# Fetching an expert's rows: one whole-row gather and a TensorE transpose, in place of four quarter-row gathers and a VectorE transpose

## The chip, the cores and the metric

The kernel runs on one core of one Trainium2 chip. The metric is the device time of one execution in microseconds (us). A profile is taken of a separate execution of the same program; its times are counted from the first instruction of that execution.

## What is computed

Three stages follow each other: attention, a gated mlp, and a mixture of eight experts of which every token uses two. The change touches only the way in which the third stage gets its rows. Cut to what matters:

```python
x = attention(q, k, v)                              # 2304 tokens x 512
x = (silu(x @ w_gate) * (x @ w_val)) @ w_out        # gated mlp, 512 -> 1536 -> 512
noisy = x @ g_gate + log1p(exp(x @ g_noise)) * noise
top2, top2_w = the two largest of 8 per token, softmax of the two
for e in range(8):
    for k in range(2):
        mask = top2[:, k] == e
        h = maximum(x[mask] @ w1[e], 0)             # 512 -> 1024
        out[mask] += top2_w[mask, k] * (h @ w2[e])  # 1024 -> 512
```

## The kernel before

TensorE (PE) multiplies in float32r. For the accuracy of float32 every operand is split into a high and a low part (`split`, L397: ScalarE copies the high part, VectorE subtracts it from the source for the low part), and three of the four products are summed (`PASSES`, L459).

The gated mlp goes through 6 blocks of 384 tokens and 12 chunks of 128 hidden columns (the loop at L763). Attention and the routing of finished blocks are woven between its matmuls. `m_evac` (L499) scales a finished block and writes its rows to the DRAM tensor `x1d`; ScalarE writes them with the columns permuted (L505). `routing` (L519) computes the gates of a block, gives each token a slot for each of its two experts, and scatters token number and weight to the DRAM list `slotd` (L607). Blocks 0 to 4 are read back from `x1d` in quarters and transposed by VectorE (`quarters`, L513); the last block is still in SBUF and is transposed by TensorE (L528), four 128x128 transposes a tile.

The experts follow (L818 on). Each has 5 tiles of 128 slots (`CAPT`): a group of 3 and a group of 2 (`GN`). A unit is one expert, one group and one of 8 hidden chunks: 16 units an expert, 128 in all. In a unit TensorE does 12 matmuls of `x_h` (L820) for its own chunk and then those of `x_o` (L835) for the chunk before: 9 with three tiles, 6 with two. A finished group is scaled and added to `out` by an indirect DMA a tile (L847).

The rows of expert e+1 are fetched while expert e is multiplied. Counted in units of expert e: at 0 `load_info` reads the slot list from DRAM; at 2 `info` turns it into row numbers; at 3 to 7 `gather` (L699) fetches one tile each; at 10 to 14 `xtrans` (L707) transposes one tile each and splits it into `XG`, which `x_h` reads. Experts 0 and 1 are fetched in part before the last block has been routed (`early_steps`, L746), and their fifth tile at the end of it (L879). Expert 7 has no expert after it, so nothing is gathered while it runs.

Transposing a tile by 32x32 blocks, as VectorE does, is a whole transpose only if each quarter of the columns stands in its own 32 partitions. So `gather` sees `x1d` as four times as many rows of 128 columns (`x1q`, L66) and fetches each tile in four indirect DMAs, with row numbers 4 x token + quarter (`idq`, L693), which need a list of their own in another layout (`inq`, four DMAs at L685). Where a line says `pin`, the instruction is kept behind everything that its engine was given before; the others may be moved by the compiler's scheduler.

The indirect DMAs are issued by GpSimd (POOL), plain loads by SyncE (SP). TensorE, VectorE (DVE) and ScalarE (ACT) each take their instructions in order.

Of the kernel before, what the change touches and what calls it, by code (L numbers as in the profile page):

```python
# [8 lines left out]
F32 = mybir.dt.float32  # L9
F32R = mybir.dt.float32r  # L10
BF16 = mybir.dt.bfloat16
I32 = mybir.dt.int32
U32 = mybir.dt.uint32
AF = mybir.ActivationFunctionType
OP = mybir.AluOpType
# [6 lines left out]
def attention_moe_kernel(ctx: ExitStack, tc: tile.TileContext, q, k, v, w_gate, w_val, w_out,  # L22
# [42 lines left out]
    x1d = dram.tile([NT + PAD, DM], F32, name="x1d")  # L65
    x1q = x1d.rearrange("t (a c) -> (t a) c", a=4)  # L66
    slotd = dram.tile([E * REG, 2], F32, name="slotd")
# [28 lines left out]
    iota8 = const.tile([P, E], F32, name="iota8")  # L96
    quad4 = const.tile([P, 1], F32, name="quad4")
    payload = const.tile([P, NTILE, 2, 2], F32, name="payload")
# [9 lines left out]
    def more_consts():  # L108
        for a in range(4):
            nc.gpsimd.memset(quad4[a * ST:(a + 1) * ST], float(a))  # L110
        nc.gpsimd.memset(wgn, 0.0)
        nc.gpsimd.memset(up, 1.0)
        sel(up, [[1, P]], 0, -1, 0.0, OP.is_gt)
        nc.gpsimd.memset(ones, 1.0)
        nc.gpsimd.iota(iota8, pattern=[[1, E]], base=0, channel_multiplier=0,
                       allow_small_or_imprecise_dtypes=True)
        nc.gpsimd.iota(payload[:, :, :, 0], pattern=[[P, NTILE], [0, 2]], base=PAD, channel_multiplier=1,
                       allow_small_or_imprecise_dtypes=True)
        nc.gpsimd.iota(base, pattern=[[REG, E]], base=0, channel_multiplier=0,
                       allow_small_or_imprecise_dtypes=True)  # L120
        nc.gpsimd.iota(basea, pattern=[[REG, E]], base=NTA, channel_multiplier=0,
                       allow_small_or_imprecise_dtypes=True)
        ini = hp_.tile([P, NROW, 2], F32, name="ini", tag="x1", bufs=X1B)
        inits.append(ini)
        inii = hp_.tile([P, NROW], I32, name="inii", tag="xf", bufs=3)
        nc.gpsimd.iota(inii, pattern=[[1, NROW]], base=0, channel_multiplier=NROW % PAD)
        nc.vector.tensor_scalar(inii, inii, PAD - 1, None, op0=OP.bitwise_and)
        nc.vector.memset(ini, 0.0)
        nc.vector.tensor_copy(ini[:, :, 0], inii)
# [18 lines left out]

    # ------------------------------------------------------------- attention + gated mlp
    p1 = ctx.enter_context(ExitStack())  # L150
# [122 lines left out]

    # local heads: a tile holds 64 queries of two heads, one under the other
    def a_scores(qd):
# [117 lines left out]

    # ---- weights of the gated mlp, as exact sums of two float32r parts
    W = {}
# [103 lines left out]
    def m_evac(j):  # L499
        for t in range(3):  # L500
            if j == NBLK - 1:
                x = p2a[0].tile([P, DM], F32, name="xrow", tag="xrow", bufs=6)
            else:
                x = hp_.tile([P, DM], F32, name="x1", tag="x1", bufs=X1B)
            nc.scalar.mul(x.rearrange("p (a m j) -> p m a j", a=4, j=ST),  # L505
                          ACC[j][t].rearrange("p (m a j) -> p m a j", a=4, j=ST), 0.5)
            r0 = PAD + (3 * j + t) * P
            nc.scalar.dma_start(out=x1d[r0:r0 + P, :], in_=x)
            if j == NBLK - 1:
                X1[j, t] = x  # L510

    # rows of x1 with a quarter of the columns to each 32 partitions, transposed by blocks
    def quarters(dst, src):  # L513
# [5 lines left out]
    def routing(j):  # L519
        L = rt.tile([P, 3, 2 * E], F32, name="L", tag="L", bufs=2)  # L520
        pl = at_tile("ps_l", 3, P)
        for t in range(3):
# [15 lines left out]
            for kk in range(KD):  # L538
                nc.tensor.matmul(pl[kk * ST:(kk + 1) * ST, t, :], wgn[:, j == NBLK - 1, kk, :], xt[:, kk, :],
                                 start=True, stop=True)  # L540
# [129 lines left out]
    GN, GT = (3, 2), (0, 3)  # L670
    INFO, IDX, IDQ, XG, XR, WX = {}, {}, {}, {}, {}, {}
    p2a, p2b = [None], [None]
# [4 lines left out]
    def load_info(e, t0, t1):  # L677
# [4 lines left out]
        nc.sync.dma_start(out=inf[:, :n, :], in_=slotd[r0:r0 + n * P, :].rearrange("(t p) c -> p t c", p=P))  # L682
        inq = rt.tile([P, 4 * CAPT], F32, name="inq", tag="inq", bufs=2)
        for a in range(4):
            nc.sync.dma_start(out=inq[a * ST:(a + 1) * ST, :4 * n],  # L685
                              in_=slotd[r0:r0 + n * P, 0:1].rearrange("(g i) o -> i (g o)", i=ST))
        LI[e, t0] = inf, ids, inq, n

    def info(e, t0):
        inf, ids, inq, n = LI.pop((e, t0))  # L690
        idq = rt.tile([P, 4 * CAPT], I32, name="idq", tag="idq", bufs=3)
        pin(nc.vector.tensor_copy(ids[:, :n], inf[:, :n, 0]))
        pin(nc.vector.tensor_scalar(idq[:, :4 * n], inq[:, :4 * n], 4.0, quad4, op0=OP.mult, op1=OP.add))  # L693
        for t in range(t0, t0 + n):
            IDQ[e, t] = idq[:, 4 * (t - t0):4 * (t - t0 + 1)]
            INFO[e, t] = inf[:, t - t0, :]
            IDX[e, t] = ids[:, t - t0:t - t0 + 1]

    def gather(e, t, rows=NT):  # L699
        x = p2a[0].tile([P, 4, P], F32, name="xrow", tag="xrow", bufs=6)  # L700
        for g in range(4):
            nc.gpsimd.indirect_dma_start(  # L702
                out=x[:, g, :], out_offset=None, in_=x1q[:4 * (PAD + rows), :],
                in_offset=bass.IndirectOffsetOnAxis(ap=IDQ[e, t][:, g:g + 1], axis=0))
        XR[e, t] = x

    def xtrans(e, t):  # L707
# [5 lines left out]
        hi, lo = XG[e, g][:, :, 0, c0:c0 + P], XG[e, g][:, :, 1, c0:c0 + P]  # L713
        xt = hp_.tile([P, KD, P], F32, name="xgT", tag="xf", bufs=3)
        pin(quarters(xt, x))
        split(hi, lo, xt)

# [45 lines left out]
    for i, (j, c) in enumerate(seq):  # L763
# [37 lines left out]
        pend.append((j, c))  # L801
    # ------------------------------------------------------------- experts
    for _ in early[0]:
# [71 lines left out]
    def route_step():  # L875
# [6 lines left out]
        if rts and next(rts[0], "end") == "end":  # L882
# [3 lines left out]
            late.append(0)  # L886
            # tiles of slots that each expert needs
            cnt = rt.tile([P, E], F32, name="cnt")
# [25 lines left out]

    # ------------------------------------------------------------- what the static slots don't hold
    ov = ctx.enter_context(tc.tile_pool(name="ov", bufs=1, reuse_waits="tile"))
    worst = nc.values_load(ntile[0:1, E:E + 1], min_val=0, max_val=NTILE)
    with tc.If(worst > CAPT):
        for e in range(E):
            last = nc.values_load(ntile[0:1, e:e + 1], min_val=0, max_val=NTILE)  # L920
            with tc.For_i(CAPT, last, 1) as t:
# [7 lines left out]
                                             in_offset=bass.IndirectOffsetOnAxis(ap=ids, axis=0))  # L929
                xn = ov.tile([P, DM], F32, name="o_xn")  # L930
                nc.vector.tensor_copy(xn.rearrange("p (m a j) -> p m a j", a=4, j=ST),
                                      x.rearrange("p (a m j) -> p m a j", a=4, j=ST))
                ps = ps_at.tile([P, DM], F32, name="o_ps", tag="at")
                for kk in range(KD):
                    nc.tensor.transpose(ps[:, kk * P:(kk + 1) * P], xn[:, kk * P:(kk + 1) * P], ident)
                xt = ov.tile([P, DM], F32, name="o_xt")
# [47 lines left out]
```

## Time and profile before

| what | us |
|---|---|
| device time, median of 3 runs | 1088.91 (1087.77 to 1089.51) |
| span of the profiled execution (no other time of it is given) | 1189.3 |
| TensorE matmuls busy in it | 1079.4 (91%) |
| VectorE busy | 580.1 (49%) |
| ScalarE busy | 439.4 (37%) |
| GpSimd busy | 366.0 (31%) |
| last matmul ends at; from there to the end of the span | 1175.5; 13.8 |

The span of the profiled execution is 100.4 us longer than the median of the timed ones, so an idle stretch in the profile need not be there in the time. The page has the busy time of each engine, the span in 40 slices, the DMA queues, the chain of work that ended last, and the costliest groups of instructions; the trace behind it answers for a line, a tile, or a stretch of time. Busy times of TensorE have modelled ends, and consecutive matmuls overlap in them: the step from one start to the next is what one costs in a stream.

### The profile page before, as it was taken

The numbers are of one execution on the slowest core, as the hardware profiler recorded it, in microseconds if no ns is written. First come the engines' busy times: TensorE is split into PE (matmuls) and PEld (weight loads), VectorE is DVE, ScalarE is ACT, GpSimd is POOL, SyncE is SP. The second block draws the span as 40 slices with busy tenths as digits, with TensorE's granted clock in tenths as the row PEclk, the third lists the DMA queues.
The fourth block names the chain that finished last, engine by engine and source line by source line (L and its number), as shares of the span: only waits on it lengthen the run. The fifth ranks groups of instructions, "written<-read, shape, count | busy, mean of one in ns | idle before, by whom it ended". The sixth has DMA issues, their size and how long they took to land.

```text
span 1189.3 us, 17431 instructions
## 1 busy us (share of the span) xinstructions
PE 1079.4 (91%) x6262; PEld 935.6 (79%) x6268; DVE 580.1 (49%) x1524; ACT 439.4 (37%) x1099; POOL 366.0 (31%) x418
## 2 busy tenths in 40 slices
PE   7988799999999999999889688897979799897995
PEld 4667688988888888898878577796969688696994
DVE  5879885555556645535455162341606153250511
ACT  4645454245444534434333141331505042241410
POOL 5136420311212300200343616234252615334211
PEclk8989899999999999999989889898979999898998
DMA  8666763565426313114452254351715444351412
GB/s 170 157 181 184 207 166 95 87 210 140 74 60 131 49 49 96 40 45 147 90 164 72 41 128 97 77 140 36 180 42 142 85 103 115 58 160 31 63 14 35
DMA packets 187154, 123.65 MB, mean 104 GB/s; under 512 B 96225, under 2 KB 154081, under 8 KB 187057
## 3 DMA queue, kind: packets, MB, share of 16 engines
q1 hardware_dynamic: 168256, 92.22, 30.2%
q0 software_dynamic: 16208, 25.49, 11.7%
q10 hardware_dynamic: 2592, 4.72, 1.1%
q8 instruction: 51, 0.84, 0.3%
q14 instruction: 47, 0.38, 0.1%
HBM read 98.04 MB, written 24.30 MB: 103 GB/s over the span
## 4 chain that ended last, share of the span: by engine, by line
PE 29%; issue 13%; DMA 3%; POOL 3%; another core or an unknown queue 1%; DVE 1%; SPq 1%; ACT 0%; POOLq 0%; DVEq 0%; ACTq 0%
PE acc L835 14%; PE ps_h L820 14%; POOL xrow L702 2%; DMA out_dram<-y,ids 2%; DMA slotd<-payload,si 1%; POOL slotd L607 1%; DMA raw<-in_moe_w_dram 0%; POOL out_dram L847 0%; SPq L685 0%; PE ps_g L467 0%; PE ps_v L467 0%; DVE W L399 0%; DVE wohl L399 0%; DMA inf<-slotd 0%
## 5 line engine op out<-in xcount | busy, mean ns | idle before, releaser
L835 PE MATMUL acc<-W,hhl 128*128 128x512 f32 x960 | 262.3, 417 | 39.2 <-issue 34.4
L820 PE MATMUL ps_h<-xg,W 128*128 128x256 f32 (+1 forms) x1536 | 260.0, 316 | 21.7 <-issue 21.7
L820 PEld LDWEIGHTS ps_h<-xg,W 128*128 128x128 f32 x1536 | 244.4, 194 | 38.3 <-issue 26.8
L835 PEld LDWEIGHTS acc<-W,hhl 128*128 128x128 f32 x960 | 187.0, 202 | 76.6 <-issue 37.9
L824 DVE SCALAR_TENSOR_TENSOR hhl<-ps_h,hhl 128x256 fp32r<-128x256 f32 (+1 forms) x128 | 61.5, 480 | 297.0 <-ACT hhl L823 207.3
L702 POOL DMA_INDIRECT xrow<-x1d,idq x160 | 154.0, 963 | 102.2 <-issue 55.8
L467 PE MATMUL ps_g<-xh,W 128*128 128x384 f32 x864 | 170.8, 345 | 5.9 <-DVE th L475 5.9
L823 ACT ACTIVATE hhl<-ps_h 128x256 fp32r<-128x256 f32 (+1 forms) x128 | 55.8, 436 | 323.9 <-PE ps_h L820 145.7
L467 PE MATMUL ps_v<-xh,W 128*128 128x384 f32 x864 | 168.9, 343 | 5.1 <-DVE th L482 5.1
L494 PE MATMUL acc<-wohl,hhl 128*128 128x512 f32 x648 | 171.3, 405 | 0.0
L467 PEld LDWEIGHTS ps_g<-xh,W 128*128 128x128 f32 x864 | 152.9, 191 | 13.9 <-DVE th L475 6.5
L467 PEld LDWEIGHTS ps_v<-xh,W 128*128 128x128 f32 x864 | 152.3, 190 | 8.0 <-DVE th L482 3.7
L847 POOL DMA_INDIRECT out_dram<-y,ids x40 | 62.9, 1573 | 257.6 <-ACT y L846 234.8
L494 PEld LDWEIGHTS acc<-wohl,hhl 128*128 128x128 f32 x648 | 120.4, 191 | 25.4 <-issue 3.0
L398 ACT CAST W<-raw 128x512 fp32r<-128x512 f32 x128 | 76.2, 618 | 59.2 <-PE acc L835 36.1
L399 DVE TENSOR_TENSOR W<-raw,W 128x512 fp32r<-128x512 f32 x128 | 85.4, 687 | 25.2 <-ACT W L398 14.6
L607 POOL DMA_INDIRECT slotd<-payload,si x36 | 36.3, 1010 | 130.5 <-DVE si L594 100.4
L398 ACT CAST hhl<-th 128x384 fp32r<-128x384 f32 x72 | 36.9, 513 | 96.7 <-DVE th L482 95.1
L227 POOL DMA_DIRECT2D v<-in_v_dram x28 | 19.4, 695 | 165.9 <-PE ps_o L332 153.4
L475 DVE SCALAR_TENSOR_TENSOR th<-th,ps_g 128x384 f32<-128x384 f32 x72 | 39.7, 551 | 51.7 <-ACT th L474 43.9
L474 ACT ACTIVATE th<-ps_g 128x384 f32<-128x384 f32 x72 | 35.3, 490 | 79.7 <-PE ps_g L467 69.9
L304 ACT ACTIVATE sc<-sc,mn 126x126 f32<-126x126 f32 (+3 forms) x152 | 56.5, 374 | 20.8 <-DVE mn L301 20.6
(136 smaller groups left out, 1018.9 us busy)
## 6 DMA issues: line engine op xcount, KB each, us to landing
raw<-in_moe_w_dram SPq DMA_DIRECT2D x128, 256.0 KB
raw<-wod SPq DMA_DIRECT2D x60, 256.0 KB
raw<-in_moe_w_gate_dram SPq DMA_DIRECT2D x12, 512.0 KB
raw<-in_moe_w_val_dram SPq DMA_DIRECT2D x12, 512.0 KB
raw<-in_moe_w_out_dram SPq DMA_DIRECT2D x12, 512.0 KB
out_dram<-zero SPq DMA_DIRECT2D x20, 256.0 KB
x1d<-x ACTq DMA_DIRECT2D x15, 256.0 KB
xq<-x1d SPq DMA_DIRECT2D x60, 64.0 KB
```

Source lines behind the costliest of these rows:

```text
L304: nc.scalar.activation(s[:n, i, :m], s[:n, i, :m], AF.Exp, bias=mn[:n, i:i + 1], scale=-1.0, accum_out=rs[:n, i])
L398: nc.scalar.copy(dst_hi, src)
L399: (eng or nc.vector).tensor_tensor(dst_lo, src, dst_hi.bitcast(F32), op=OP.subtract)
L467: nc.tensor.matmul(ps, W[c][:, o + a, kk * P:(kk + 1) * P], XH[j, kk][:, b2, :], start=(kk == KORD[0] and a == 0 and b2 == 0), stop=(kk == ...
L494: nc.tensor.matmul(ACC[j][t], h[:, a, t * P:(t + 1) * P], wo[:, b2, :], start=(c == 0 and a == 0 and b2 == 0), stop=(c == NC1 - 1 and a == 1))
L607: s = nc.gpsimd.indirect_dma_start(out=slotd, out_offset=bass.IndirectOffsetOnAxis(ap=si[:, t, i:i + 1], axis=0), in_=pay[:, t, i, :], in_ ...
L702: nc.gpsimd.indirect_dma_start(out=x[:, g, :], out_offset=None, in_=x1q[:4 * (PAD + rows), :], in_offset=bass.IndirectOffsetOnAxis(ap=IDQ[ ...
L820: nc.tensor.matmul(ps, w[:, a, kk * P:(kk + 1) * P], XG[e, g][:, kk, b2, :], start=(kk == 0 and a == 0 and b2 == 0), stop=(kk == KD - 1 an ...
L823: nc.scalar.activation(h[:, 0, :n], ps, AF.Relu)
L824: nc.vector.scalar_tensor_tensor(h[:, 1, :n], ps, 0.0, h[:, 0, :n].bitcast(F32), op0=OP.max, op1=OP.subtract)
L835: nc.tensor.matmul(ACC2[e, g][t], h[:, a, t * P:(t + 1) * P], w[:, 2 + b2, :], start=(c == 0 and a == 0 and b2 == 0), stop=(c == NC2 - 1 a ...
L847: s = nc.gpsimd.indirect_dma_start(out=out, out_offset=bass.IndirectOffsetOnAxis(ap=IDX[e, ti], axis=0), in_=y, in_offset=None, compute_op ...
```

## The change

`x1d` now holds plain rows. `gather` fetches the 128 rows of a tile whole, 2 KB each, in one indirect DMA, with the token numbers that `info` already makes for the scatter. `xtrans` transposes the tile on TensorE, four 128x128 transposes into one PSUM bank, pinned behind what TensorE was given before; `split` then reads PSUM in place of SBUF. The second list (`inq`, `idq`, `quad4`) and its DMAs are gone. The two layouts of the gate weights (`wgn`) change places, because the read-back of blocks 0 to 4 in quarters now meets plain rows and the last block's too are plain. The branch for slots beyond five tiles (L918 on) loses a copy. The diff, without comment lines:

```diff
-    x1q = x1d.rearrange("t (a c) -> (t a) c", a=4)
...
@@ m_evac
-            nc.scalar.mul(x.rearrange("p (a m j) -> p m a j", a=4, j=ST),
-                          ACC[j][t].rearrange("p (m a j) -> p m a j", a=4, j=ST), 0.5)
+            nc.scalar.mul(x, ACC[j][t], 0.5)
@@ routing
-                nc.tensor.matmul(pl[kk * ST:(kk + 1) * ST, t, :], wgn[:, j == NBLK - 1, kk, :], xt[:, kk, :],
+                nc.tensor.matmul(pl[kk * ST:(kk + 1) * ST, t, :], wgn[:, j < NBLK - 1, kk, :], xt[:, kk, :],
@@ load_info
-        inq = rt.tile([P, 4 * CAPT], F32, name="inq", tag="inq", bufs=2)
-        for a in range(4):
-            nc.sync.dma_start(out=inq[a * ST:(a + 1) * ST, :4 * n],
-                              in_=slotd[r0:r0 + n * P, 0:1].rearrange("(g i) o -> i (g o)", i=ST))
-        LI[e, t0] = inf, ids, inq, n
+        LI[e, t0] = inf, ids, n
@@ info
-        idq = rt.tile([P, 4 * CAPT], I32, name="idq", tag="idq", bufs=3)
         pin(nc.vector.tensor_copy(ids[:, :n], inf[:, :n, 0]))
-        pin(nc.vector.tensor_scalar(idq[:, :4 * n], inq[:, :4 * n], 4.0, quad4, op0=OP.mult, op1=OP.add))
@@ gather
-        x = p2a[0].tile([P, 4, P], F32, name="xrow", tag="xrow", bufs=6)
-        for g in range(4):
-            nc.gpsimd.indirect_dma_start(
-                out=x[:, g, :], out_offset=None, in_=x1q[:4 * (PAD + rows), :],
-                in_offset=bass.IndirectOffsetOnAxis(ap=IDQ[e, t][:, g:g + 1], axis=0))
+        x = p2a[0].tile([P, DM], F32, name="xrow", tag="xrow", bufs=6)
+        nc.gpsimd.indirect_dma_start(out=x, out_offset=None, in_=x1d[:PAD + rows, :],
+                                     in_offset=bass.IndirectOffsetOnAxis(ap=IDX[e, t], axis=0))
@@ xtrans
-        xt = hp_.tile([P, KD, P], F32, name="xgT", tag="xf", bufs=3)
-        pin(quarters(xt, x))
-        split(hi, lo, xt)
+        ps = at_tile("ps_xg", KD, P)
+        for m in range(KD):
+            pin(nc.tensor.transpose(ps[:, m, :], x[:, m * P:(m + 1) * P], ident))
+        split(hi, lo, ps)
@@ the branch for slots beyond five tiles
-                xn = ov.tile([P, DM], F32, name="o_xn")
-                nc.vector.tensor_copy(xn.rearrange("p (m a j) -> p m a j", a=4, j=ST),
-                                      x.rearrange("p (a m j) -> p m a j", a=4, j=ST))
...
-                    nc.tensor.transpose(ps[:, kk * P:(kk + 1) * P], xn[:, kk * P:(kk + 1) * P], ident)
+                    nc.tensor.transpose(ps[:, kk * P:(kk + 1) * P], x[:, kk * P:(kk + 1) * P], ident)
```

## Rows read from the trace of the kernel before

**Rows 1.** Page, part 1: busy us (share of span) and instructions.
```profile
PE 1079.4 (91%) x6262; PEld 935.6 (79%) x6268; DVE 580.1 (49%) x1524; ACT 439.4 (37%) x1099; POOL 366.0 (31%) x418
```

**Rows 2.** Stages: stretch, length, busy by engine (instructions), granted clock, DMA share, GB/s.
```profile
160.00:560.00 400.00, 399.73 (x2545) 348.56 (x2543) 219.54 (x689) 175.14 (x480) 67.06 (x88) 1.00 0.39 97
590.00:629.80 39.80, 34.14 (x157) 30.35 (x156) 22.12 (x41) 14.79 (x29) 19.73 (x19) 0.87 0.54 156
629.80:711.60 81.80, 64.01 (x349) 55.09 (x349) 29.95 (x87) 22.50 (x44) 30.89 (x30) 0.87 0.34 76
...
1050.30:1118.40 68.10, 60.71 (x313) 53.48 (x312) 24.31 (x45) 19.16 (x37) 26.90 (x25) 0.92 0.32 71
1118.40:1175.10 56.70, 56.70 (x318) 51.63 (x318) 9.36 (x18) 9.27 (x20) 7.79 (x5) 1.00 0.19 24
1175.10:1189.30 14.20, 0.43 (x2) 0.01 (x1) 0.75 (x1) 0.48 (x1) 3.11 (x2) 0.68 0.31 43
```

**Rows 3.** Timeline inside a burst of gathers: start, us, instruction, [idle before, releaser].
```profile
1080.30 0.49 ACT L823 ACTIVATE hhl<-ps_h 128x384 fp32r<-128x384 f32 x1 [11.29 <-remote]
...
1085.60 0.95 POOL L702 DMA_INDIRECT xrow<-x1d,idq  x1 [0.30 <-issue]
1086.62 0.33 PE L820 MATMUL ps_h<-xg,W 128*128 128x384 f32 x1 [1.11 <-issue]
```

**Rows 4.** Timeline of TensorE around the transposes of the last block.
```profile
629.79 0.41 PE L820 MATMUL ps_h<-xg,W 128*128 128x384 f32 x1
630.04 0.60 PE L528 MATMUL ps_xt<-ident,xrow 128*128 128x128 f32 x4
630.39 2.34 PE L820 MATMUL ps_h<-xg,W 128*128 128x384 f32 x12
...
633.02 1.09 PE L528 MATMUL ps_xt<-ident,xrow 128*128 128x128 f32 x8
633.87 0.78 PE L820 MATMUL ps_h<-xg,W 128*128 128x384 f32 x3
```

**Rows 5.** Line L528: duration ns min/median/max; then its stretch, as in Rows 2.
```profile
L528 PE MATMUL ps_xt<-ident,xrow x12: 272/272/328, 630.0 to 633.8; 128*128 128x128 f32 x12
```
```profile
627.80:634.30 6.50, 6.50 (x45) 5.39 (x44) 4.41 (x8) 3.10 (x6) 2.83 (x3) 1.00 0.65 200
```

**Rows 6.** Groups by line and form: busy us, mean ns, idle before and its releaser.
```profile
L514 DVE STREAM_TRANSPOSE xgT<-xrow 128x512 f32<-128x512 f32 x40 | 28.1, 703 | 0.8 <-issue 0.8
L399 DVE TENSOR_TENSOR xg<-xgT,xg 128x512 fp32r<-128x512 f32 x40 | 27.4, 686 | 4.0 <-ACT xg L398 3.0 <-issue 0.7
L398 ACT CAST xg<-xgT 128x512 fp32r<-128x512 f32 x40 | 24.6, 617 | 12.2 <-DVE xgT L514 12.2
L529 DVE COPY x1T<-ps_xt 128x512 f32<-128x512 f32 x3 | 2.1, 686 | 2.1 <-PE ps_xt L528 2.1
L505 ACT ACTIVATE xrow<-acc 128x512 f32<-128x512 f32 x3 | 1.7, 600 | 1.0 <-PE acc L494 1.0
```

**Rows 7.** Lines L702, L847 and L685: duration ns min/median/max, first and last start.
```profile
L702 POOL DMA_INDIRECT xrow<-x1d,idq x160: 944/947/1418, 591.1 to 1085.6; - x160
```
```profile
L847 POOL DMA_INDIRECT out_dram<-y,ids x40: 1548/1560/1637, 685.3 to 1177.7; - x40
```
```profile
L685 SPq DMA_DIRECT2D inq<-slotd x40: 312/488/1116, 586.5 to 929.1; - x40
```

**Rows 8.** Timeline at the fifth tile of expert 0, last to be routed.
```profile
659.75 0.23 DVE L693 TENSOR_SCALAR idq<-inq,quad 128x4 int32<-128x4 f32 x1 [1.45 <-DMA inq<-slotd]
...
664.06 0.95 POOL L702 DMA_INDIRECT xrow<-x1d,idq  x1 [0.30 <-issue]
...
666.76 0.71 DVE L514 STREAM_TRANSPOSE xgT<-xrow 128x512 f32<-128x512 f32 x1 [0.80 <-issue]
...
668.18 0.39 PE L820 MATMUL ps_h<-xg,W 128*128 128x256 f32 x1 [0.80 <-issue]
```

**Rows 9.** Timeline of VectorE: the first transpose of expert 7's tiles.
```profile
1106.50 0.70 DVE L514 STREAM_TRANSPOSE xgT<-xrow 128x512 f32<-128x512 f32 x1
```

More of the change, by code (lines that the diff above doesn't have):

```diff
@@ L96, in attention_moe_kernel @@
     iota8 = const.tile([P, E], F32, name="iota8")
-    quad4 = const.tile([P, 1], F32, name="quad4")
     payload = const.tile([P, NTILE, 2, 2], F32, name="payload")
@@ L108, in more_consts @@
     def more_consts():
-        for a in range(4):
-            nc.gpsimd.memset(quad4[a * ST:(a + 1) * ST], float(a))
         nc.gpsimd.memset(wgn, 0.0)
@@ L670, in attention_moe_kernel @@
     GN, GT = (3, 2), (0, 3)
-    INFO, IDX, IDQ, XG, XR, WX = {}, {}, {}, {}, {}, {}
+    INFO, IDX, XG, XR, WX = {}, {}, {}, {}, {}
     p2a, p2b = [None], [None]
@@ L682, in load_info @@
         nc.sync.dma_start(out=inf[:, :n, :], in_=slotd[r0:r0 + n * P, :].rearrange("(t p) c -> p t c", p=P))
-        inq = rt.tile([P, 4 * CAPT], F32, name="inq", tag="inq", bufs=2)
-        for a in range(4):
-            nc.sync.dma_start(out=inq[a * ST:(a + 1) * ST, :4 * n],
-                              in_=slotd[r0:r0 + n * P, 0:1].rearrange("(g i) o -> i (g o)", i=ST))
-        LI[e, t0] = inf, ids, inq, n
+        LI[e, t0] = inf, ids, n
     def info(e, t0):
-        inf, ids, inq, n = LI.pop((e, t0))
-        idq = rt.tile([P, 4 * CAPT], I32, name="idq", tag="idq", bufs=3)
+        inf, ids, n = LI.pop((e, t0))
         pin(nc.vector.tensor_copy(ids[:, :n], inf[:, :n, 0]))
-        pin(nc.vector.tensor_scalar(idq[:, :4 * n], inq[:, :4 * n], 4.0, quad4, op0=OP.mult, op1=OP.add))
         for t in range(t0, t0 + n):
-            IDQ[e, t] = idq[:, 4 * (t - t0):4 * (t - t0 + 1)]
             INFO[e, t] = inf[:, t - t0, :]
```

## The prediction

> **What bounds the kernel now.** I read the busy table first: TensorE is busy 1079.4 of 1189.3 us and no other engine over half of the span [rows 1]. Busy matmuls overlap, so this alone does not make TensorE the bound; the stages do. From 160 to 560 us, in the gated mlp, TensorE is busy 399.7 of 400.0 us at the full clock [rows 2]. The last expert runs 56.7 us, from 1118.4 to 1175.1, busy in all of it and again at the full clock [rows 2]. The reader should set this last expert beside the six before it: they do the same 16 units with the same matmuls, and take 406.8 us from 711.6 to 1118.4, 67.8 each [rows 2]. What they have and the last has not is the fetch of the next expert's rows.
>
> The timeline inside one of them shows where the 11 us go. POOL issues 20 gathers (25 instructions in the stage, 5 in the last expert's [rows 2]), the last at 1085.6, 1.25 us from one to the next (0.95 and 0.30 of issue [rows 3]). In the second half of this burst and just behind it ScalarE stands 11.3 us with a cause that the profile can't name, and TensorE does single matmuls with 1.1 us of "issue" before them [rows 3]. The granted clock of the stage falls to 0.92 with it [rows 2]. So the profile suggests that the bursts are the thing to remove, and the change removes three quarters of them.
>
> The timed runs say otherwise, and this is the main choice that I make. The span profiled is 1189.3, the median of the timed runs 1088.9, 100.4 less; the profiled execution has no other time than its span. Count what the stalls cost in the profile. Experts 1 to 6: 406.8 - 6 x 56.7 = 66.6 us. Expert 0: 81.8 - 56.7 = 25.1, less some 3 us of routing that it really does (an estimate: 12 transposes at 0.107 are 1.3, and the gate matmuls behind them about as much again). The end of the mlp, 590 to 629.8, where the first gathers fall: 39.8 - 34.1 = 5.7 idle, and 13% of 34.1, 4.4, for the clock of 0.87 [rows 2]. The sum is 99 us, against the 100.4 by which the timed runs are shorter. The stretch before 560 can't supply it, since TensorE has no idle time to give up there. So I take the stalls to be almost wholly absent from the timed runs: there TensorE is the bound from the mlp to the last expert, at 56.7 us an expert, and only what is added to or taken from TensorE's stream counts. The Trainium skill has a mechanism that would fit (NOTIFIC — the notification-queue block, section 7.1): the path that carries an engine's trace records can hold the engine back. No run here shows it so far.
>
> **The change part by part.**
>
> Transposes added to TensorE. 8 experts x 5 tiles x 4 = 160 transposes of 128x128. The kernel already does this operation, in the same type and from the same kind of tile, on the last block: four start between a matmul of x_h at 629.79 and the next at 630.39, and eight take from 633.02 to 633.87 [rows 4]. That is 0.85 / 8 = 0.106 us each. In the first case the step is 0.60. One matmul of x_h is in it: twelve take 2.34 [rows 4], the last of them 0.33 [rows 3], so a step is 2.01 / 11 = 0.18. That leaves 0.42 for four, 0.105 each, the change of weights included. I take 0.107: 160 x 0.107 = 17.1 us, all of it on the path, since the stream of the last expert has no gaps to take it in [rows 2]. The duration in the trace, 272 ns [rows 5], is the upper bound (43.5 us); zero, if gaps take it all, is the lower. The steps are nearest, being the very operation in the very stream.
>
> That the data come from a gather and not from ScalarE adds a wait on TensorE: the four stand in its queue, in order, and behind them all the following matmuls. The data have time: the last gather of a burst is issued at 1085.6, the first transpose of that expert runs at 1106.5, and by then all five tiles are there [rows 3, 9]. With a quarter of the DMAs they land earlier still. I take 0; if the cover were gone it would cost what the gather is late, once an expert.
>
> VectorE loses 40 transposes of 0.703 us, 28.1 us [rows 6]; hidden today, so 0. The split reads PSUM: ScalarE's copy of a 128x512 tile takes 600 ns from PSUM against 617 from SBUF, VectorE's 686 against 686 for its subtraction [rows 6], so 0 too. The PSUM bank comes from a pool of three which in this stage only the last routing shares; tiles come one in a unit, so a bank is long free.
>
> POOL loses 160 gathers and gets 40. One with 128 indices of 512 B takes 0.947 us, one with 128 rows of 2 KB and an addition 1.56 [rows 7]: 40 x 0.95 to 40 x 1.56, 38 to 62 us for 151.5. Queued behind them are the scatters to out, which no engine waits for until the end of the kernel, and the last expert gathers nothing: 0. SP loses 40 small loads of 0.488 us (median) [rows 7], among the weight loads: 0.
>
> The fifth tile of expert 0 is the one place where the gather is on the path. VectorE waits 1.45 us for the second list, the fourth gather is issued at 664.06, the transpose starts at 666.76, and TensorE stood 0.80 us before its matmul at 668.18 [rows 8]. The change takes off the 1.45 and three gathers of 1.25. It gives back that TensorE now does the transposes itself and must then wait for ScalarE's high part, some 0.6 + 0.6 us that VectorE's 0.70 and the same copy took before. Between -2 and +2 us; I take 0.
>
> Moves with one answer: the scaling of a block with plain columns (same size), the exchanged gate weights (same loads and matmuls), the branch beyond five tiles (not entered in the trace): 0.
>
> **Sum.** Made on the profile, without what the bursts do: 1189.3 + 17.1. The timed runs lack those 100 us, and TensorE's addition is the same: 1088.9 + 17.1 = 1106.0.
>
> **The rivals.**
>
> *The bursts stall the timed runs too* (faster). If part of the 100 us is in the timed time, and the stall goes with the number of gathers, three quarters of that part are gained. It decides at 17.1 / 0.75 = 23 us of stalls; with a third of the 100, 33, the time is 1088.9 + 17.1 - 25 = 1081. For it: the profile shows the stalls so plainly. Against it: the sum above leaves room for 1 or 2 us, and for more only if the first 160 us of the kernel are also longer in the profile. Chance 0.10.
>
> *A transpose costs its duration.* 160 x 0.272 = 43.5, 1132. The Trainium skill (TensorE: Matmul & The Clock Gate, Part 4: PE-mode transpose) gives about 275 ns for one in a kernel; by this figure, an estimate, 160 are 44 us and the time 1133. The trace has the same figure as a duration but 0.107 as a step, so little is left for it [rows 4, 5]. The clock stayed at 1.00 in that stretch [rows 5]. Chance 0.03.
>
> *TensorE waits in front of the transposes*: for the gather's landing, a semaphore, or because the pin keeps matmuls behind that the scheduler had ahead. One wait of 0.3 us a tile is 40 x 0.3 = 12 us: 1118; one of 2 us an expert is as much. For it: the instructions behind stand still, which VectorE's wait did not cause. Against it: 20 us of lead. Chance 0.10.
>
> *The transposes are hidden*: the timed stream has gaps, for instance from weights that come late, or VectorE's 28 us come free where it holds TensorE. Then nothing changes, 1089. Against it: the last expert's stream has no gap [rows 2]; it prepares no weights, which leaves this a chance of 0.06.
>
> That the change does not do what it says can be left out: 160 gathers become 40 by the text of the loop.
>
> **How the numbers follow.** Likeliest, 0.71: 1102 to 1111, the transposes added, the fifth tile's two us either way, small waits. The range goes to the waiting rival above, 1119, and below into the first one, 1094, where some 16 us of stalls would be in the timed runs: 1094 to 1119. About 0.2% is what a measurement of this kernel can tell from no change (2.2 us). Slower by more than that: 0.71 + 0.03 + 0.10 and a little of the first rival, 0.85. Same: 0.06. Faster: 0.09.
>
> **What the profile of the changed kernel would show.** 160 more transposes at steps of 0.107 us between matmuls of x_o and x_h; 40 gathers of 0.95 to 1.6 us on POOL; only 15 block transposes on VectorE. The last expert stays at 56.7 us. Experts 1 to 6 can't go under 56.7 + 20 x 0.107 = 58.8, and should come down towards it from 67.8, as the bursts shrink: so the profiled span falls, to some 1130, while the timed time rises. If both fall, the stalls were real and the first rival holds. Idle time of TensorE before the new transposes, released by a gather, would show the waiting rival; a step of 0.27 the second.

## The result

The changed kernel takes 1098.1 us (median of 4 runs, 1096.3 to 1099.8), the kernel before 1088.5 on the same chip (1087.8 to 1089.5). That is 9.7 us more, a ratio of 1.0095 on record (the two medians alone give 1.0089), with a 95% interval of 1.0078 to 1.0112. Forecast were 1106, in a range of 1094 to 1119; the time lies in the range, but below its likeliest part, 1102 to 1111. So the change is slower, by a little over half of what the sum gave. The profiled execution took 1097.7, its span is 1095.9: 1.8 us lie around the span. What recording costs can't be read from this: every timed run of the changed kernel has a span and a granted clock on record, so none is known to have gone unrecorded.

One thing must be said ahead, because without it the numbers behind can't be read. The kernel before has two times, and they go with the chip: 1088.5 us on the chip of the result and 1086.0 on another that was met later (the record doesn't number the first, so they may be one), 1184 to 1185 on three others, where one run of 1329.2 us at a mean granted clock of 0.74 is left out. No chip was met at two times, so the chip itself and the time at which it was met are not told apart. The profile of before that stands ahead of the prediction is of the second sort, by its span of 1189.3 us and by its stages; the times beside it are of the first. I call chips with the second time holding chips, for what their profiles show. The changed kernel takes 1095 to 1098 on both sorts.

The profile after, from the result's chip. First the busy table of its page (busy us, share of the span, instructions), which answers [rows 1]:

```profile
PE 1055.1 (96%) x6422; PEld 927.1 (85%) x6428; DVE 554.6 (51%) x1474; ACT 440.5 (40%) x1099; POOL 248.4 (23%) x294
```

160 matmuls more on TensorE, 40 + 10 instructions less on VectorE, 120 + 4 less on POOL. The stages, with the columns of [rows 2]: block 5 of the mlp, expert 0, the first and the last of experts 1 to 6, expert 7, and what follows the last matmuls:

```profile
531.70:619.10 87.40, 83.74 (x452) 76.44 (x451) 50.55 (x116) 39.85 (x74) 11.41 (x11) 0.96 0.48 147
619.10:680.30 61.20, 60.39 (x373) 53.33 (x372) 25.96 (x79) 23.03 (x44) 15.64 (x14) 1.00 0.36 97
680.30:737.90 57.60, 57.60 (x334) 52.33 (x333) 22.14 (x40) 20.63 (x40) 12.65 (x10) 1.00 0.50 119
...
968.80:1026.60 57.80, 57.80 (x333) 52.78 (x332) 19.92 (x36) 18.53 (x36) 12.69 (x10) 1.00 0.36 83
1026.60:1083.60 57.00, 57.00 (x319) 51.45 (x318) 9.35 (x18) 9.65 (x20) 7.82 (x5) 1.00 0.19 24
1083.60:1095.90 12.30, 0.06 (x1) 0.00 (x0) 0.75 (x1) 0.10 (x1) 3.11 (x2) 0.66 0.35 48
```

The 67.8 us that experts 1 to 6 took on the mean in the profile before have become 57.7, TensorE is busy in all of them and the clock stays at 1.00. The new transposes in TensorE's timeline (start, us, instruction), which answer [rows 4]:

```profile
718.96 1.58 PE L807 MATMUL ps_h<-xg,W 128*128 128x256 f32 x12
720.38 1.54 PE L822 MATMUL acc<-W,hhl 128*128 128x512 f32 x6
721.76 0.60 PE L702 MATMUL ps_xg<-ident,xrow 128*128 128x128 f32 x4
722.11 1.66 PE L807 MATMUL ps_h<-xg,W 128*128 128x256 f32 x12
723.61 1.56 PE L822 MATMUL acc<-W,hhl 128*128 128x512 f32 x6
```

From one x_o to the next the unit takes 723.61 - 720.38 = 3.23 us with four transposes; the unit ahead of it, without, 720.38 - 717.57 = 2.81 (the x_o before that starts at 717.57). The difference is 0.42 for four, or 0.105 each. The groups by line (busy us, mean ns, idle before and releaser), which answer [rows 6, 7]:

```profile
L689 POOL DMA_INDIRECT xrow<-x1d,ids x40 | 38.9, 973 | 73.7 <-issue 44.3 <-PE ps_xg L702 24.2 <-DVE ids L682 5.2
...
L395 DVE TENSOR_TENSOR xg<-ps_xg,xg 128x512 fp32r<-128x512 f32 x40 | 27.4, 684 | 5.6 <-ACT xg L394 5.6
...
L702 PE MATMUL ps_xg<-ident,xrow 128*128 128x128 f32 x160 | 24.0, 272 | 0.0
...
L394 ACT CAST xg<-ps_xg 128x512 fp32r<-128x512 f32 x40 | 23.2, 580 | 5.8 <-PE ps_xg L702 5.8
```

A gather of whole rows costs POOL 0.973 us, hardly more than one of quarter rows, and the split from PSUM costs the same as from SBUF. TensorE is never idle before a transpose (0.0). In the whole second half it waits twice:

```profile
PE ps_v L463 <- DVE th L478: 3.6, 1, 3.6
PE ps_r L576 <- DVE cm L572: 0.8, 1, 0.8
```

### The profile page after: what moved, and what is told of

Its sections match the earlier page's. It is cut to its first block, busy times and chain, and to the rows that moved or that the text cites. A ratio compares the mean times of both kernels' runs of the same rounds, so it can differ in the third digit from the quotient of the medians.

```text
span 1095.9 us, 17496 instructions
## 1 busy us (share of the span) xinstructions
PE 1055.1 (96%) x6422; PEld 927.1 (85%) x6428; DVE 554.6 (51%) x1474; ACT 440.5 (40%) x1099; POOL 248.4 (23%) x294
## 3 DMA queue, kind: packets, MB, share of 16 engines
q0 software_dynamic: 14288, 25.49, 12.4%
## 5 line engine op out<-in xcount | busy, mean ns | idle before, releaser
L807 PE MATMUL ps_h<-xg,W 128*128 128x256 f32 (+1 forms) x1536 | 249.3, 311 | 0.0
L822 PE MATMUL acc<-W,hhl 128*128 128x512 f32 x960 | 240.9, 391 | 0.0
L807 PEld LDWEIGHTS ps_h<-xg,W 128*128 128x128 f32 x1536 | 232.2, 188 | 8.0 <-issue 0.4
L822 PEld LDWEIGHTS acc<-W,hhl 128*128 128x128 f32 x960 | 174.7, 188 | 28.8
L490 PE MATMUL acc<-wohl,hhl 128*128 128x512 f32 x648 | 170.3, 404 | 0.0
L463 PE MATMUL ps_g<-xh,W 128*128 128x384 f32 x864 | 168.4, 342 | 0.4 <-DVE th L471 0.4
L490 PEld LDWEIGHTS acc<-wohl,hhl 128*128 128x128 f32 x648 | 121.2, 192 | 23.2 <-issue 2.0
L395 DVE TENSOR_TENSOR W<-raw,W 128x512 fp32r<-128x512 f32 x128 | 83.2, 687 | 51.8 <-ACT W L394 51.3
L394 ACT CAST W<-raw 128x512 fp32r<-128x512 f32 x128 | 73.7, 618 | 65.3 <-PE acc L822 46.0
L478 DVE TENSOR_TENSOR th<-th,ps_v 128x384 f32<-128x384 f32 x72 | 39.6, 551 | 45.7 <-PE ps_v L463 45.7
L395 DVE TENSOR_TENSOR wohl<-raw,wohl 128x512 fp32r<-128x512 f32 x60 | 41.3, 688 | 32.9 <-ACT wohl L394 32.7
```

The costliest lines, as they stand in the source:

```text
L394: nc.scalar.copy(dst_hi, src)
L395: (eng or nc.vector).tensor_tensor(dst_lo, src, dst_hi.bitcast(F32), op=OP.subtract)
L463: nc.tensor.matmul(ps, W[c][:, o + a, kk * P:(kk + 1) * P], XH[j, kk][:, b2, :], start=(kk == KORD[0] and a == 0 and b2 == 0), stop=(kk == ...
L478: nc.vector.tensor_tensor(t, t, ps, op=OP.mult)
L490: nc.tensor.matmul(ACC[j][t], h[:, a, t * P:(t + 1) * P], wo[:, b2, :], start=(c == 0 and a == 0 and b2 == 0), stop=(c == NC1 - 1 and a == 1))
L807: nc.tensor.matmul(ps, w[:, a, kk * P:(kk + 1) * P], XG[e, g][:, kk, b2, :], start=(kk == 0 and a == 0 and b2 == 0), stop=(kk == KD - 1 an ...
```

## The experiments

**The kernel before again, and each half of the change alone.** These four ran on one holding chip.

> The kernel before, unchanged, for a second profile. The changed kernel is 9.7 us slower, not 17.1; three theories share these first four runs. Theory 1 (bursts): the bursts of 20 gathers hold TensorE in the timed runs of before too, by some 7 us, and the change gives that back. Theory 2 (price): a transpose costs about 0.06 us in the timed stream, not 0.107. Theory 3 (VectorE): the 28 us that VectorE no longer spends, or another order of instructions, give 7 us back. All three: 1088.5, ratio 1.000. If the profile of before is long by its recording alone, its span is again near 1189; if it was a chance of that one execution, the span is near 1087 and shows where 7 us go: theory 1 wants them in the bursts of experts 0 to 6, about 1 us each.

Measured: 1184.7 us (ratio 1.0004, 0.9978 to 1.0029), where before's other runs gave 1185.4. All three theories had 1088.5 for it. Its stages, expert 2 and expert 4:

```profile
777.50:846.00 68.50, 61.05 (x314) 53.72 (x313) 25.17 (x47) 20.51 (x40) 26.91 (x25) 0.93 0.44 104
...
914.50:981.00 66.50, 58.63 (x314) 51.77 (x313) 25.17 (x47) 20.51 (x40) 26.90 (x25) 0.95 0.45 104
```

They are those of [rows 2], and here the timed runs are as long as the profiled one (1188.7). The timeline of expert 6 shows the hold again:

```profile
1068.66 2.25 PE L820 MATMUL ps_h<-xg,W 128*128 128x384 f32 x12
...
1077.15 0.49 ACT L823 ACTIVATE hhl<-ps_h 128x384 fp32r<-128x384 f32 x1 [9.89 <-remote]
...
1077.70 2.48 PE L835 MATMUL acc<-W,hhl 128*128 128x512 f32 x9 [2.62 <-issue]
...
1084.86 0.48 PE L820 MATMUL ps_h<-xg,W 128*128 128x384 f32 x1 [1.61 <-issue]
...
1086.27 0.48 PE L820 MATMUL ps_h<-xg,W 128*128 128x384 f32 x1 [0.92 <-issue]
```

ScalarE's instruction has its input when the matmuls of x_h from 1068.66 on are done, at 1070.9; it starts at 1077.15. TensorE's x_o, which needs its result, starts 0.06 us after it ends. From about 1081 to 1088 TensorE then does single matmuls. The trace names no cause for ScalarE's wait or for these. The granted clock falls as well (columns of [rows 2]), so a part of what the hold costs is work at a lower clock behind it:

```profile
1078.00:1082.00 4.00, 3.10 (x13) 2.16 (x12) 0.24 (x1) 0.00 (x0) 3.09 (x4) 1.00 0.23 65
1082.00:1086.00 4.00, 0.96 (x2) 0.57 (x2) 0.00 (x0) 0.00 (x0) 2.21 (x3) 0.60 0.19 50
...
1090.00:1094.00 4.00, 4.00 (x16) 3.24 (x15) 0.56 (x1) 0.33 (x1) 0.00 (x0) 0.62 0.00 0
```

The second kernel takes out the transposes of TensorE:

```diff
-        ps = at_tile("ps_xg", KD, P)
-        for m in range(KD):
-            pin(nc.tensor.transpose(ps[:, m, :], x[:, m * P:(m + 1) * P], ident))
-        split(hi, lo, ps)
+        xt = hp_.tile([P, KD, P], F32, name="xgT", tag="xf", bufs=3)
+        pin(quarters(xt, x.rearrange("p (g c) -> p g c", g=4)))
+        split(hi, lo, xt)
```

> The change without TensorE's transposes: one whole-row gather a tile, and VectorE's transpose by blocks of 32 as before. Left out: blocks are not put in their places, so experts multiply wrongly ordered data; the work is the same. Theory 1: 1088.5 - 7.4 = 1081. Theory 2: 1088.5. Theory 3: 1088.5 by VectorE's time; lower only if the order is what helps.

Measured: 1079.9 us. One gather a tile and the chip holds nothing; the experts run in 55.5 us:

```profile
619.30:678.10 58.80, 57.99 (x348) 51.42 (x348) 29.03 (x86) 22.75 (x44) 15.49 (x14) 1.00 0.40 103
...
955.50:1011.00 55.50, 55.50 (x314) 50.79 (x313) 24.22 (x44) 19.04 (x37) 12.69 (x10) 1.00 0.38 87
```

The third takes out the gather instead: `inq`, `idq` and `x1q` stay as in the kernel before, and the transposes write the quarters where they belong:

```diff
-            pin(nc.tensor.transpose(ps[:, m, :], x[:, m * P:(m + 1) * P], ident))
+            pin(nc.tensor.transpose(ps[:, :, m * ST:(m + 1) * ST], x[:, m, :], ident))
```

> The change without its gather: four quarter-row gathers a tile from the second list, as before, then four transposes on TensorE that write the quarters to their places in PSUM. Theory 1: 1088.5 + 17.1 = 1105.6, or 7.4 over the changed kernel. Theories 2 and 3: 1098, as the changed kernel.

Measured: 1208.6 us, 24 more than before on this chip (ratio 1.0212, 1.0173 to 1.0251). Transposes alone give the loss and none of the gain. The loss is 7 us larger than 160 transposes at 0.107; expert 2, with the four gathers a tile kept, takes 3.3 us more than the 68.5 above, at a lower granted clock (0.90 for 0.93):

```profile
783.10:854.90 71.80, 61.31 (x333) 54.34 (x333) 22.18 (x41) 20.51 (x40) 26.89 (x25) 0.90 0.42 96
```

The fourth does every transpose twice (`for m in range(2 * KD)`, taken modulo 4):

> The changed kernel with each of its 160 transposes done twice into the same place. Theories 1 and 3: 160 x 0.107 more, 1098.1 + 17.1 = 1115. Theory 2: 1098.1 + 9.7 = 1108.

Measured: 1112.1 us. Experts 1 to 6 take 59.8 us on the mean (686.7 to 1045.5 by the first matmul of each), against 57.7 with single transposes and 55.5 with none:

```profile
746.60:806.30 59.70, 59.70 (x353) 54.67 (x352) 22.61 (x40) 20.62 (x40) 12.70 (x10) 1.00 0.48 115
```

So 20 more transposes cost 2.1 to 2.3 us an expert, twice over: 0.104 to 0.113 each. Theory 2, a cheaper transpose, falls. Theory 3, VectorE's time, falls with the third kernel, which freed VectorE as the changed one does. That the bursts hold TensorE is shown for this chip, at a far larger price than theory 1 had (some 100 us, not 7). Whether they also cost 7 us on the result's chip was not yet answered.

**What of the gathers holds the engines.** These four met another holding chip.

> The changed kernel, unchanged, beside a run of before on the same chip. In the first four runs before took 1185.4 and not 1088.5, so there are chips on which the bursts hold TensorE and chips on which they hardly do; with one gather a tile the kernel took 1080 on the former. Theory 1 (bursts): the changed kernel takes 1097 on either sort of chip; the ratio to before is 0.926 where before takes 1185, and 1.009 where it takes 1088. Theory 2 (price of a transpose under 0.107) alone: where before takes 1185 the changed kernel takes 1195.

Measured: 1094.9 us against 1184.5 for before: 0.9253 (0.9219 to 0.9288). On such a chip the change gains 7.5%.

The next has four quarter-row gathers without the second list; their row numbers are 4 x token + quarter, worked out on VectorE:

```diff
+        for g in range(4):
+            pin(nc.vector.tensor_scalar(idq[:, :n, g], inf[:, :n, 0], 4.0, float(g), op0=OP.mult, op1=OP.add))
...
-        nc.gpsimd.indirect_dma_start(out=x, out_offset=None, in_=x1d[:PAD + rows, :],
-                                     in_offset=bass.IndirectOffsetOnAxis(ap=IDX[e, t], axis=0))
+        for g in range(4):
+            nc.gpsimd.indirect_dma_start(
+                out=x[:, g * P:(g + 1) * P], out_offset=None, in_=x1q[:4 * (PAD + rows), :],
+                in_offset=bass.IndirectOffsetOnAxis(ap=IDQ[e, t][:, g:g + 1], axis=0))
```

> The changed kernel with four quarter-row gathers a tile, their row numbers worked out on VectorE from the first list, so that the second list and its loads are gone. On a chip where before takes 1185: if the number of gathers holds TensorE, 1205, as with the list; if the small loads of the second list do, 1098. Where before takes 1088: 1105 and 1098.

Measured: 1209.1 us. The second list and its small loads are acquitted; it is the gathers.

Then I tried to spread them, by their place in the program alone:

```diff
-    GA, XA = (3, 4, 5, 6, 7), (10, 11, 12, 13, 14)
+    GA, XA = (3, 5, 7, 9, 11), (10, 11, 12, 13, 15)
```

> The kernel before with the five tiles of experts 2 to 7 gathered in units 3, 5, 7, 9 and 11 in place of 3 to 7 (the fifth transposed in unit 15), so that POOL pauses some 3 us after every four gathers. If the hold needs an unbroken burst of over some 10 us: six of the eight bursts go, 1185 - 6 x 12.3 = 1111 where before takes 1185, and 1088 or a few less where it takes 1088. If it is a cost of each gather, unchanged.

Measured: 1184.6 us (0.9999, 0.9979 to 1.0018). This run says nothing on the theory, since the edit did not do what it says: the first and the last gather of a burst are still 19 steps of 1.25 us apart, because the row numbers of all five tiles are ready at once and nothing keeps POOL from going on.

```profile
1057.01 1.00 POOL L702 DMA_INDIRECT xrow<-x1d,idq  x1 [3.81 <-DVE idq L693]
...
1080.86 0.95 POOL L702 DMA_INDIRECT xrow<-x1d,idq  x1 [0.30 <-issue]
```

Two half-row gathers a tile (as the kernel with four, with `a=2`):

> The changed kernel with two half-row gathers a tile: 10 gathers in a burst, 80 in all. Where before takes 1185: a cost of each gather gives about 1098 + a third of the 107 between one and four gathers a tile, 1134; a hold that begins only after some 10 us of unbroken gathers gives 1098 to 1105, since ten last 12.5 us. Where before takes 1088: 1098 to 1101.

Measured: 1112.2 us, 17 over the changed kernel. The largest piece, 7 us, stands in expert 0 (68.2 for 61.2), where six scatters of the slot list end 5 us ahead of the ten gathers; experts 1 to 6 take 58.2 on the mean, half a us more than with one gather a tile; the rest lies ahead of the experts and at the kernel's end:

```profile
619.90:688.10 68.20, 63.48 (x372) 55.62 (x371) 26.41 (x83) 22.91 (x44) 20.11 (x19) 0.95 0.33 87
...
921.20:979.50 58.30, 58.30 (x334) 52.79 (x333) 22.29 (x42) 20.61 (x40) 17.42 (x15) 1.00 0.46 118
```

Ten gathers in a row cost 0.5 us, twenty cost 12.3 (67.8 - 55.5). That is no price for each gather. But the time met neither forecast, 1134 for a price and 1098 to 1105 for a hold that begins after some 10 us.

**The bursts broken up, and both sorts of chip.** The paced kernel is the kernel before with the row numbers of each tile made by a VectorE instruction at that tile's unit, so that POOL must wait for it (it also gives the early tiles more room):

```diff
-        pin(nc.vector.tensor_scalar(idq[:, :4 * n], inq[:, :4 * n], 4.0, quad4, op0=OP.mult, op1=OP.add))
...
+        idq, inq = IDQ[e, t]
+        pin(nc.vector.tensor_scalar(idq, inq, 4.0, quad4, op0=OP.mult, op1=OP.add))
         for g in range(4):
...
-    GA, XA = (3, 4, 5, 6, 7), (10, 11, 12, 13, 14)
+    GA, XA = (3, 5, 7, 9, 12), (8, 10, 12, 14, 15)
```

> The kernel before, VectorE's transposes kept, its quarter gathers really spread: e7's edit left the order on POOL as it was, since the row numbers of all five tiles were ready at once and the scheduler issued 20 gathers in one go again. Here the numbers of each tile are worked out by a VectorE instruction of its own at its unit (3, 5, 7, 9, 12), so that four gathers of 5 us follow each other and then POOL rests some 3 us; expert 0's tiles come three slots apart, expert 1's two units. If the hold needs an unbroken burst of 10 us: where before takes 1185 it goes to about 1080 to 1095, where before takes 1088 to 1080 or a little over. If each gather has its price, or the rate over 30 us sets it: within 20 us of 1185.

This met a chip that does not hold: 1091.1 us against 1086.0 (1.0056, 1.0035 to 1.0078). Nothing to gain there, and the early tiles' new places cost 4 us in block 5.

> The kernel before once more, for its profile on the chip of this call. Where it takes 1185: as the first one, 67 to 68 us for experts 1 to 6. Where it takes 1088: the first theory wants 8 us of holds in the bursts, so experts 1 to 6 at 56.5 in place of 55.5.

Measured: 1083.4, with a span of 1081.6. This is the profile of before that the prediction lacked. Block 5, expert 0, the first and last of experts 1 to 6, expert 7, the end:

```profile
532.10:615.90 83.80, 80.95 (x436) 72.33 (x434) 51.79 (x121) 39.17 (x74) 26.31 (x25) 1.00 0.52 150
615.90:677.10 61.20, 58.71 (x349) 51.20 (x349) 28.80 (x85) 22.78 (x44) 30.66 (x29) 1.00 0.36 85
677.10:732.60 55.50, 55.50 (x313) 50.66 (x312) 25.68 (x49) 20.50 (x41) 28.89 (x26) 1.00 0.61 138
...
955.30:1011.00 55.70, 55.70 (x314) 50.57 (x313) 24.29 (x45) 19.14 (x37) 26.90 (x25) 1.00 0.38 87
1011.00:1068.10 57.10, 57.09 (x319) 51.64 (x317) 9.36 (x18) 9.72 (x20) 7.79 (x5) 1.00 0.19 24
1068.10:1081.60 13.50, 0.00 (x0) 0.00 (x0) 0.75 (x1) 0.03 (x1) 3.12 (x2) 0.67 0.31 44
```

The same 20 gathers an expert (x25 with the five scatters) and no hold at all: 55.65 us an expert from 677.1 to 1011.0, 0.15 over the kernel with one gather a tile. Theory 1 falls for this sort of chip; the 7 us are elsewhere.

> The paced kernel met a chip on which the quarter gathers hold nothing (before 1086 there). Once more, for a chip of the other sort: where before takes 1185, a hold that needs an unbroken burst of 10 us gives 1085 to 1100, one that is set by the rate over 30 us or by each gather gives 1165 to 1190. Where before takes 1086: 1091 again.

The paced kernel once more, now on a third holding chip: 1115.1 us against 1183.9 (0.9434, 0.9381 to 0.9487). The stages of expert 0, where 20 gathers still come in one go, and of experts 2 and 4, where they come in fours; behind them POOL in expert 1, at the end of one group of four and the start of the next two:

```profile
625.90:708.00 82.10, 65.15 (x343) 55.55 (x344) 30.87 (x91) 21.65 (x42) 31.18 (x31) 0.85 0.30 67
...
763.70:819.80 56.10, 56.05 (x314) 50.54 (x313) 25.80 (x52) 20.82 (x40) 28.87 (x26) 1.00 0.54 123
...
875.50:931.30 55.80, 55.80 (x314) 50.56 (x313) 25.84 (x51) 20.73 (x41) 28.28 (x26) 1.00 0.52 124
```

```profile
727.44 0.94 POOL L704 DMA_INDIRECT xrow<-x1d,idq  x1 [0.30 <-issue]
731.93 0.94 POOL L704 DMA_INDIRECT xrow<-x1d,idq  x1 [3.55 <-DVE idq L702]
...
740.26 0.95 POOL L704 DMA_INDIRECT xrow<-x1d,idq  x1 [3.64 <-DVE idq L702]
```

Same number of gathers, same bytes, same chip sort: 55.8 us an expert for 67.8. What holds the engines on such a chip is the 20 in one go, as in expert 0 of this same execution. The pauses also spread the 20 gathers over some 41 us in place of 25, so a limit on an unbroken run and one on the gathers within such a stretch are not told apart. The total of 1115 missed the forecast of 1085 to 1100 by expert 0 (82.1 for 60.2 on the chip that holds nothing) and block 5 (91.8 for 87.7).

> The changed kernel, for its profile and time beside before on the chip of this call. Where before takes 1086: +9.8 us, a ratio of 1.009, made of +17.1 for the transposes, -2.6 in expert 0, -2.4 in blocks 1 to 4 of the mlp and -1.9 behind the last matmul; experts 1 to 6 at 57.7, against 55.65 in before. Where before takes 1185: 1095, 0.925, with the same stages.

Measured: 1095.6 us against 1183.9, 0.9266 (0.9225 to 0.9307), with experts 1 to 6 at 57.7 once more.

## Why the prediction was right, and where it was not

**The bound.** Right for the chip that was timed: without holds TensorE is busy in all of experts 1 to 6, before and after. The step by which I came to it was wrong in its reason. I summed the stalls to 99 us, saw 100.4 us between the span and the timed runs, and put the stalls down to the profiled execution. The sum was near (set beside the later profile of before, experts 1 to 6 lose 72.9 us, expert 0 20.6 and block 5 9.6, 103 in all), but the difference lay between two chips. On the holding ones the stalls are in every timed run. I also took 56.7 us as an expert's clean time; expert 7 does a seventeenth x_o of six matmuls, and the clean time is 55.5 to 55.65, so that the floor of 58.8 that I set for the changed kernel was 1.1 us too high.

The sentence of the Trainium skill that I put beside it (NOTIFIC — the notification-queue block, section 7.1) is neither borne out nor ruled out. The profile of before on the chip that holds nothing is recorded too and shows no hold. But no run is known to have gone unrecorded, and the traces of the two sorts of chip differ. For the kernel before, the chip that holds nothing left 16743 records of semaphore changes (the counters by which engines and DMAs tell that they are done) and the first holding chip of the experiments 13612; for the changed kernel, which holds on neither, the result's chip left 14190 and the second holding chip 13327. The median time from a gather's issue to its landing, which is worked out from such records, is the last number of the first row, from the chip that holds nothing, and can't be given in the second, from a holding one:

```profile
xrow<-x1d,idq POOLq DMA_INDIRECT x160, 2.5
```

```profile
xrow<-x1d,idq POOLq DMA_INDIRECT x160
```

So on holding chips a wait without a name may be one whose record is missing. Whether the missing records and the holds have one cause is open; the time of an execution without recording on a holding chip would tell.

**The transposes.** Right, to the digit that counts. Forecast 0.107 us each and 17.1 in all; measured 0.105 in one unit, 0.104 from the experts of before and after (57.72 - 55.65 = 2.07 for 20), 0.104 for the doubled ones, 0.11 against the second kernel, which has the same gathers (57.7 - 55.5). That makes 16.6 to 18 for 160. The duration that the trace gives is 272 ns here as in [rows 5]; the figure of about 275 ns in the Trainium skill (TensorE: Matmul & The Clock Gate, Part 4: PE-mode transpose) agrees with the duration and would have priced the change, by this estimate of 44 us, at some two and a half times its cost.

**The wait in front of them.** Right: none. The page gives 0.0 us of idle time before L702.

**What I put at 0.** Here is most of the 7.4 us between 17.1 and 9.7. I set the profile of before on the chip that holds nothing beside that of the result, by stages; block 0 is left out, since it differs by 4 us between runs of one kernel (119.5 to 123.9 for the changed one):

| stage | before | after | difference | transposes in it, at 0.104 | rest |
|---|---|---|---|---|---|
| blocks 1 to 4 | 360.7 | 358.4 | -2.3 | 0 | -2.3 |
| block 5 | 83.8 | 87.4 | +3.6 | 16, 1.7 | +1.9 |
| expert 0 | 61.2 | 61.2 | 0 | 24, 2.5 | -2.5 |
| experts 1 to 6 | 333.9 | 346.3 | +12.4 | 120, 12.5 | -0.1 |
| expert 7 | 57.1 | 57.0 | -0.1 | 0 | -0.1 |
| end | 13.5 | 12.3 | -1.2 | 0 | -1.2 |
| sum | 910.2 | 922.6 | +12.4 | 16.6 | -4.2 |

The sum is the difference of two executions that are not known to be of one chip, at the upper end of the measured 9.7 (8.5 to 12.2 by the interval). In the two other profiles of the changed kernel block 5 took 85.9 and 86.0 and the end 11.6 and 11.4, which brings the sum to about 10. The +1.9 of block 5 goes with a granted clock of 0.96 there, 1.00 before.

- The fifth tile of expert 0. I had seen what the change takes off [rows 8], gave the transposes' handover as much back, and took 0. TensorE's idle time in expert 0 went from 2.5 us (61.2 - 58.7) to 0.8 (61.2 - 60.4), and its 24 transposes cost nothing in the end. The second kernel shows the saving by itself: it fetches as the changed one does, has no such transposes on TensorE, and takes 58.8 us there in place of 61.2. The term was mis-sized: -2.5, where -2 to +2 stood and 0 was taken.
- The end of the kernel. I costed nothing there. POOL's closing wait for its DMA queue is shorter by 1.3 us: 3.542 us before and 2.235 after (duration ns min/median/max, the longest is meant):

```profile
L980 POOLq DRAIN  x3: 46/103/3542, 1077.2 to 1081.3; - x3
```

```profile
L964 POOLq DRAIN  x3: 46/103/2235, 1092.9 to 1095.7; - x3
```

Every profile with 160 gathers has 3.54 or 3.62 us here and every one with 40 has 2.23. It does not simply go with their number, though: the kernel with 80 half-row gathers has the longest wait. The cause is open.

```profile
L971 POOLq DRAIN  x3: 46/103/5257, 1103.9 to 1109.7; - x3
```

- Blocks 1 to 4 of the mlp, where the change touches only the scaling of a finished block and the layout of its gate weights. The matmuls are as many, and TensorE is busy throughout in both; here the first of the four:

```profile
171.40:258.70 87.30, 87.30 (x536) 76.73 (x536) 49.19 (x150) 36.82 (x98) 17.08 (x24) 1.00 0.45 119
```

```profile
173.30:260.00 86.70, 86.68 (x536) 76.48 (x535) 49.24 (x150) 36.76 (x98) 17.08 (x24) 1.00 0.47 118
```

Every kernel with one gather a tile has 86.7 there, every one with two or four 87.1 to 87.9. Those with two or four are scaled and routed as before in some and as after in others, so neither makes the 0.6 us. The order of TensorE's matmuls doesn't either: by their tiles it is the same in blocks 1 to 4 of both traces. Some steps of the mlp's last product (L494, in the changed kernel L490) take 0.235 us in place of 0.226; why is open.

**The rivals.** The bursts do stall timed runs, by some 98 us (1184 for 1086) and not 33, on three of the chips met; on two of them the changed kernel was timed too and is faster by 7.3 to 7.5%. Had the time before come from such a chip, the forecast would have been wrong in sign: no holds in the timed runs was true of the timed chip alone, and that it was this one was luck. The low end of the range, too, I had drawn for stalls in the timed runs; the measured time lies near it without any, by the small terms above. The waits and the hidden transposes did not come.

**The marks to look for.** The last expert stayed at 57, experts 1 to 6 came down to 57.7, with 40 gathers of 0.97 us on POOL. The span was to fall to some 1130 while the time rises; it fell to 1095.9 (1091.4 and 1094.8 on two holding chips). I had the holds shrink with the number of gathers, and they went altogether, since five in a row hold nothing.

## What to carry to other kernels

Price an operation that joins a saturated TensorE stream by the step between starts where the same operation already runs, not by its duration, and look for the small places (a late tile, the end of a queue) where the removed work was not hidden. When a profiled span and the timed runs differ by 9%, don't explain the difference away before a profile and a time of one execution stand beside each other. A long unbroken run of indirect DMAs went with no loss on one chip and with 8% of the time on three others. There, breaking it up gained 5.7% and the change shown here 7.3 to 7.5%; where nothing was held, they cost 0.6% and 1.0%.

## What the runs showed of the hardware that I had not expected

On three chips a burst of 20 indirect gathers in one go (1.25 us apart, 128 rows of 512 B each) held ScalarE and TensorE from some 11 us after its start (1060.0 to 1070.9 in the first run) and cost 12.3 us an expert, a part of it by the lower granted clock behind it. Ten in a row cost 0.5 us, five nothing, and 20 in fours with pauses 0.2 (55.8 against 55.65). The DMA engines were busy for about a fifth of the time meanwhile, and POOL itself went on at its pace. On one other chip the same 20 cost 0.15 us. What the chips differ in, by which way POOL's burst reaches the other engines, and whether the recording has a part in it, stays open: no trace names what they wait for, and the traces of the holding chips lack records.

A gather of 128 rows of 2 KB takes POOL 0.973 us on the mean and one of 512 B 0.972 (both on chips that hold nothing): the rows' length hardly counts.
